# Windowed attention with a two-layer MLP: the fourth tile of keys and queries transposed by DMA instead of on the tensor engine

## Chip, cores and metric

The kernel runs on one core of a Trainium2 chip. The metric is the time of one execution on the device in microseconds, as the median of several runs. The profile is of one such execution.

## What is computed

Attention over a band of 32 tokens to either side, for 8 sequences of 576 tokens and 8 heads of 64 values; then, on the 4608 tokens with the heads side by side, a layer of width 2048 with a quick GELU, and a layer back to 512. All inputs and the output are float32.

```python
scores = scale * np.matmul(q, k.transpose(0, 1, 3, 2))          # (8, 8, 576, 576), scale 1/8
mask = np.abs(pos[:, None] - pos[None, :]) <= 32
scores = np.where(mask, scores, -1000000000.0)
attn = softmax(scores)
x = np.matmul(attn, v)                                          # then to (4608, 512)
h = x @ w_in
out = (h * (1.0 / (1.0 + np.exp(-1.702 * h)))) @ w_out
```

## The kernel before

The tokens of all sequences are one row of 4608. Keys and queries are handled in tiles of 512 tokens (the first 576 tokens are the two pieces "A" and "B", then come tiles 1, 2, 3 and so on). Attention is done in units of 128 query tokens, 36 of them, each shifted by 32 tokens, so that unit u takes queries 128u+32 to 128u+159 and keys 128u to 128u+191. The MLP takes pairs of units, 256 tokens, called t. The instructions of every engine stand in the order in which the code writes them; nothing reorders them afterwards. Each engine works through its own list and waits on semaphores.

`head()` is the opening: loads, and the attention and MLP of the first units. From `window(4)` on one window does one pair: window w computes the attention of units 2w and 2w+1, the first MLP layer of pair w-1 (`layer1(w - 1, d)`, eight pieces), and the second layer of pair w-2. Window 4 is written out by hand, since there the opening meets the steady state: it does units 7, 8 and 9, the rest of the second layer of units 4 and 5, and the first layer of pair 3.

Scores need keys and queries with the 64 values of a head on the partitions. They are held in rings: `kT`, 1536 tokens and 64 more, and `qT`, 384 columns for each of four token phases and 16 more. Tile 3 starts again at the front of the ring (token 1536 is place 0). A unit that reads over the ring's end finds the first tokens repeated behind it; these are copied there by VectorE, for queries in `queries_wrap` (L226), for keys as the tile is put in place (in `keys_T`, or by the copy at L741). Unit 11 is the first that reads tile 3, in its second block, through these repeated places.

Two ways lead into the rings:

- By TensorE (`keys_T`, `queries_T`): the tile is loaded by `load_heads`, four consecutive tokens of a head on one partition; `pair_heads` copies two heads side by side into `kc` or `qc`; `heads_T` transposes in four groups of four into one PSUM bank, and a copy (L106) puts it into the ring. Tiles A, B, 1, 2 and 3 go so.
- By DMA (`keys_X`, `queries_X`): keys are loaded by `load_keys`, a token on a partition, 128 tokens at a time, and each 128 tokens are one transposing transfer (`dma_start_transpose`) from the sync engine's queue. Queries are loaded by `load_heads`, copied by `pair_heads`, and then moved by one transposing transfer for the tile. Tiles 4 to 8 go so, issued in `feed`: in an even window the first two key transfers of a tile, in the odd window after it the query transfer and the two other key transfers.

All loads from memory go out on the queue of GpSimd, which casts to bf16. The sync engine's queue carries the stores of the output, the transposing transfers of `kT` and `qT`, and those of x (`x_T` without a bank, L315). Both queues keep their order of issue, and a transfer waits for the eighth transfer before it on its side. Staging buffers `ks` and `qs` are three deep. PSUM banks come in four kinds: two "h", one "o", four "a", one "t".

Other names used later: `odd_v(m)` copies the values of unit m shifted by half a unit, from `ve` to `vo` (two copies); `x_T(7, "t", nc.scalar)` transposes x of unit 7 on TensorE and copies it on ScalarE, and the first layer of pair 3 starts when this copy is done; `g_sums`, `product`, `keep`, `result` are the second layer of later pairs, with seven products in place of eight.

Of the kernel before, what the change touches and what calls it, by code (L numbers as in the profile page):

```python
# [22 lines left out]
JT = 4  # L23
NV = 8
RING = 1536
# [3 lines left out]
class _Kernel:  # L29
# [410 lines left out]
    def head(self):  # L440

        nc, dve, act, pool = self.nc, self.nc.vector, self.nc.scalar, self.nc.gpsimd
# [125 lines left out]
        self.load_v(8)  # L568
        self.load_v(9)
        self.load_v(10)  # L570
        for c in "kq":
            self.load_heads(3, c)
        self.layer1(2, 0)
        self.values(6)
        self.norm(6)
# [15 lines left out]
            self.load_v(m)  # L591
        self.load_keys(4)
        self.load_heads(4, "q")

    def window(self, w):
        nc, dve, sp = self.nc, self.nc.vector, self.nc.sync
        a, b = 2 * w, 2 * w + 1
        att = w < self.NW
        t, act = w - 2, nc.scalar
        l1 = [(lambda d=d: self.layer1(w - 1, d)) for d in range(8)] if w <= self.NW else []  # L600

        def run(lst, n=1):
            for _ in range(min(n, len(lst))):
                lst.pop(0)()

        def loads():
            for m in (2 * w + 6, 2 * w + 7):
                if m < self.NU:
                    self.load_v(m)
            if w % 2 == 0 and 512 * (w // 2 + 3) < self.N:  # L610
                self.load_keys(w // 2 + 3)
                self.load_heads(w // 2 + 3, "q")

        if w == 4:
            l2 = [(lambda u=u, i=i: self.layer2(u, i, "oh"[u % 2], (dve, act)[u % 2])) for u in (4, 5) for i in range(4)]
            self.scores(7)
            self.scores(a)
            run(l2, 3)
            self.band(7)
            self.scores(b)  # L620
            run(l2)
            self.band(a)
            self.values(7, "th")
            self.gelu_table()
            for m in (10, 11):
                self.odd_v(m, act)
            self.band(b)
            self.norm(7)
            run(l2, 2)
            self.values(a)  # L630
            self.values(b)
            run(l2)
            self.x_T(7, "t", nc.scalar)
            self.norm(a)
            self.x_T(a)
            self.norm(b)
            self.x_T(b)
            run(l2)
            loads()
            run(l1, 2)  # L640
            for c in "qk":
                for hp in range(4):
                    self.pair_heads(c, 3, hp, dve)
            run(l1, 2)
            for hp in range(4):
                self.keys_T(3, hp)
                self.queries_T(3, hp, "a", nc.scalar)
                run(l1)
            self.g_sums(w - 1, 0)
            self.feed(w)  # L650
            return
        loads()
        if not att:
            self.close(w, l1)
            return
        self.scores(a)
        if w > 5:
            self.scores(b)
        self.g_sums(t, 1, (0, 1))
        self.product(t, 1, "o")  # L660
        self.keep(t, 1, dve)
        self.product(t, 2, "h")
        if w == 5:
            self.scores(b)
        self.g_sums(t, 1, (2, 3))
        self.result(t, 11)
        self.gelu_table()
        self.product(t, 5, "t")
        self.band(a)
        self.product(t, 6)  # L670
        self.band(b, 0)
        self.keep(t, 6, dve)
        self.band(b, 1)
        run(l1)
        self.values(a)
        self.values(b)
        self.norm(a)
        self.x_T(a)
        self.product(t, 7)
        self.keep(t, 7, dve)  # L680
        self.result(t, 22)
        run(l1, 1)
        self.product(t, 4)
        self.result(t, 21, act)
        self.norm(b)
        self.x_T(b)
        self.product(t, 3)
        self.result(t, 12)
        run(l1, len(l1) - 4)
        self.g_sums(w - 1, 0)  # L690
        self.feed(w)
        run(l1, 4)
# [109 lines left out]
```

## Time and profile before

| | |
|---|---|
| median of 3 runs | 296.21 us (295.53 to 297.52) |
| the profiled execution | 295.53 us, of which the span from first to last instruction is 293.6 us |
| mean granted clock of TensorE | 1.000 |
| transposes in the chain, `tp L176` | 2% of the span |
| window 4, tile 3's transposes | 74.97 to 80.25 us |
| window 5, first scores | 80.25 us |

"Busy" is the time in which an engine has an instruction in work. The chain of work that ended last is followed back from the last instruction to what released each step. In lists of instructions or pieces the first number is the start and the second the duration, in us from the start of the span. SPq is the queue of the sync engine, whose entries are the issues of transfers: their duration is the issue and not the transfer; the landing time counts from the issue's start to the transfer's semaphore.

### The profile page before, as it was taken

The page shows a single profiled execution, that of the slowest core. Times are in us where ns is not written, and L with a number is a line of the kernel's source. Part 1 is how long each engine was busy: PE and PEld are TensorE (multiplying, and loading weights), DVE is VectorE, ACT ScalarE, POOL GpSimd, SP SyncE. Part 2 cuts the span into 40 slices and gives each one's busy share as a digit, 9 for nine tenths or more (in the row PEclk, how much of TensorE's full clock was granted, in tenths as well). Part 3 has the DMA queues.
Part 4 walks back from the last instruction along what each step waited for, and adds up shares of the span by engine and source line. Part 5 has one row for each costly group of instructions (what it writes and reads, how often), then busy time and mean ns, then how long its engine had stood idle before and what let it go on. Part 6 is the DMA issues. An engine that isn't in the chain of part 4 may idle for free.

```text
span 293.6 us, 9587 instructions
## 1 busy us (share of the span) xinstructions
PE 287.0 (98%) x4050; PEld 236.8 (81%) x4052; DVE 194.1 (66%) x584; ACT 189.6 (65%) x314; POOL 87.1 (30%) x127
## 2 busy tenths in 40 slices
PE   8899999999999999999999999999999999999994
PEld 3568765866888888888888888888888888888884
DVE  3662377679696858685868586858685858583352
ACT  4677457688775757575757575757575757675330
POOL 8875434977546202720252030202000000000000
PEclk9999999999999999999999999999999999999999
DMA  9999999999999993999299938791863030303012
GB/s 147 144 206 207 199 184 169 165 168 186 165 160 155 162 215 80 144 188 212 33 164 191 200 29 136 115 177 11 136 120 97 14 98 18 95 15 94 2 71 74
DMA packets 118650, 37.78 MB, mean 129 GB/s; under 512 B 96080, under 2 KB 114256, under 8 KB 118608
## 3 DMA queue, kind: packets, MB, share of 16 engines
q0 software_dynamic: 75888, 18.16, 71.9%
q1 hardware_dynamic: 42272, 18.62, 31.4%
q8 instruction: 32, 0.52, 0.7%
q10 hardware_dynamic: 448, 0.39, 0.5%
q14 instruction: 10, 0.08, 0.1%
HBM read 36.96 MB, written 9.44 MB: 158 GB/s over the span
## 4 chain that ended last, share of the span: by engine, by line
PE 93%; DVE 2%; DMA 1%; POOL 1%; issue 1%; ACT 0%; POOLq 0%; DVEq 0%
PE h_ps L332 43%; PE o_ps L394 32%; PE o_ps L344 7%; PE pv L292 4%; PE sc L263 4%; PE tp L176 2%; DMA ve<-in_v_dram 1%; PE tp L319 1%; DVE x L304 1%; POOL neg L237 0%; PE sc L245 0%; DVE o_sb L412 0%; POOL ve L157 0%; DVE kT L106 0%; ACT qT L106 0%
## 5 line engine op out<-in xcount | busy, mean ns | idle before, releaser
L332 PE MATMUL h_ps<-xT,w_in_sb 128*128 128x256 bf16 x1152 | 135.7, 273 | 0.0
L334 ACT ACTIVATE g<-h_ps 128x512 f16<-128x512 f32 x144 | 85.5, 595 | 73.3 <-PE h_ps L332 72.0
L332 PEld LDWEIGHTS <-w_in_sb 128*128 128x128 bf16 x1152 | 112.0, 98 | 13.4 <-issue 0.3
L157 POOL DMA_DIRECT2D ve<-in_v_dram x40 | 33.8, 855 | 99.8 <-PE pv L292 79.0
L394 PEld LDWEIGHTS <-gs 128*128 128x128 f16 x480 | 45.8, 98 | 5.8
L394 PE MATMUL o_ps<-w_sum,gs 128*128 128x256 f16 x360 | 44.3, 273 | 0.0
L269 ACT ACTIVATE p<-sc 128x512 bf16<-128x512 f32 x72 | 37.2, 603 | 2.7 <-PE sc L263 2.5
L394 PEld LDWEIGHTS <-g 128*128 128x128 f16 x360 | 34.2, 98 | 4.5 <-ACT g L334 0.2
L371 DVE TENSOR_TENSOR gs<-g 128x512 f16<-128x512 f16 x30 | 12.7, 422 | 31.6 <-ACT g L334 31.6
L304 DVE TENSOR_TENSOR x<-pv,rec 128x256 bf16<-128x256 f32 x72 | 30.6, 425 | 2.7 <-DVE rec L303 0.2
L394 PE MATMUL o_ps<-w_out_sb,g 128*128 128x256 f16 x240 | 29.0, 273 | 0.0
L412 DVE TENSOR_TENSOR o_sb<-o_ps,part 128x256 f32<-128x256 f32 x45 | 19.0, 423 | 12.0 <-PE o_ps L394 11.4
L106 DVE COPY part<-o_ps 128x256 f32<-128x256 f32 x45 | 19.1, 424 | 11.6 <-PE o_ps L394 10.3
L281 DVE TENSOR_TENSOR p<-p,mask 128x512 bf16<-128x512 bf16 x64 | 24.4, 424 | 0.6 <-ACT p L269 0.5
L344 PE MATMUL o_ps<-w_out_sb,g 128*128 128x512 f16 x96 | 23.2, 380 | 0.0
L106 DVE COPY vo<-ve 64x528 bf16<-64x528 bf16 x61 | 18.6, 305 | 3.5 <-DMA ve<-in_v_dram 2.1
L146 POOL DMA_DIRECT2D ks<-in_k_dram x22 | 18.8, 873 | 2.1 <-DMA qs<-in_q_dram 1.3
L269 ACT ACT_TABLE_LOAD x15 | 19.2, 1283 | 0.3
L431 ACT ACT_TABLE_LOAD x15 | 19.2, 1283 | 0.3
L303 DVE RECIPROCAL rec<-pv 128x4 f32<-128x4 f32 x72 | 12.6, 175 | 9.9 <-PE pv L292 9.9
L106 DVE COPY kT<-tp 128x512 bf16<-128x512 bf16 (+3 forms) x24 | 12.3, 531 | 7.3 <-PE tp L176 6.8
L292 PEld LDWEIGHTS <-p 128*64 128x64 bf16 x576 | 11.1, 110 | 6.3 <-DVE p L281 3.6
(69 smaller groups left out, 263.5 us busy)
## 6 DMA issues: line engine op xcount, KB each, us to landing
out_dram<-o_sb SPq DMA_DIRECT2D x34, 256.0 KB, 2.9
ve<-in_v_dram POOLq DMA_DIRECT2D x32, 128.0 KB, 5.9
ks<-in_k_dram POOLq DMA_DIRECT2D x19, 128.0 KB, 7.7
w_in_sb<-in_moe_w_in_dram POOLq DMA_DIRECT2D x4, 512.0 KB, 10.8
w_out_sb<-in_moe_w_out_dram POOLq DMA_DIRECT2D x4, 512.0 KB, 12.3
qs<-in_q_dram POOLq DMA_DIRECT2D x2, 448.0 KB, 11.5
qs<-in_q_dram POOLq DMA_DIRECT2D x3, 256.0 KB, 6.9
qs<-in_q_dram POOLq DMA_DIRECT2D x2, 384.0 KB, 10.8
```

The costliest lines, as they stand in the source:

```text
L106: (eng.copy if eng is self.nc.scalar else eng.tensor_copy)(out, in_)
L157: self.nc.gpsimd.dma_start(self.ve[m % NV][off:off + n, :, :self.D], self.v[b, :, s:s + n, :].rearrange("h s d -> s h d"))
L269: nc.scalar.activation(p[:, eo].rearrange("k h (s j) -> k h s j", j=JT), sc[eo].rearrange("k h (j s) -> k h s j", j=JT), AF.Exp, scale=sel ...
L281: self.nc.vector.tensor_mul(pv, pv, msk.to_broadcast([128, 4, 2, SQ]))
L292: nc.tensor.matmul(acc[half][blk * 64:blk * 64 + 64, hh, :], p[:, h % 2, h // 2 * 2 + blk, :], vt[:, h, :D + 1], start=(hh == 0), stop=(hh ...
L304: nc.vector.tensor_mul(x[:, hs, :], acc[half][:, :, :D], rec[:, hs, :].to_broadcast([128, 4, D]))
L332: nc.tensor.matmul(hps[:, i, :], self.w_in_sb[:, kr, ff * 128:(ff + 1) * 128], self.xT[t][:, kr, :], start=(i == 0 and kr == 0), stop=(i = ...
L334: nc.scalar.activation(self.g[t][:, ffs[0]:ffs[1] + 1:ffs[1] - ffs[0], :], hps, AF.Gelu_apprx_sigmoid)
L344: nc.tensor.matmul(o_ps, self.g[t][:, ff, s * 128:(s + 1) * 128], self.w_out_sb[:, ff, :], start=(ff == 0), stop=(ff == self.NFF - 1))
L394: nc.tensor.matmul(self.part[t, key], x, y, start=(first and k == 0), stop=(k == 7), skip_group_check=True)
L412: self.nc.vector.tensor_add(dst, self.part[t, src], self.part[t, other])
L431: self.nc.scalar.activation(self.spark, self.spark, AF.Gelu_apprx_sigmoid)
```

## The change

Tile 3 takes the way by DMA. Its keys are loaded by `load_keys` (five transfers on GpSimd's queue instead of two), and four transposing transfers on the sync queue, issued at the end of `head()`, put them into `kT`. Its queries are still loaded by `load_heads`; ScalarE copies them in window 4, where it had copied the values of units 10 and 11, and one transposing transfer, issued after the loads of window 4, puts them into `qT`. VectorE copies the first 64 keys behind the ring's end and then the values of units 10 and 11. TensorE's 32 transposes, the eight copies before them and the twelve after them are gone, and the eight pieces of the first layer follow one another.

```diff
@@ head()
         self.load_v(8)
         self.load_v(9)
         self.load_v(10)
-        for c in "kq":
-            self.load_heads(3, c)
+        self.load_keys(3)
+        self.load_heads(3, "q")
         self.layer1(2, 0)
...
         self.load_keys(4)
         self.load_heads(4, "q")
+        for c in range(JT):
+            self.keys_X(3, c)
@@ window(), w == 4
             self.gelu_table()
-            for m in (10, 11):
-                self.odd_v(m, act)
+            for hp in range(4):
+                self.pair_heads("q", 3, hp, act)
             self.band(b)
...
             run(l2)
             loads()
-            run(l1, 2)
-            for c in "qk":
-                for hp in range(4):
-                    self.pair_heads(c, 3, hp, dve)
-            run(l1, 2)
-            for hp in range(4):
-                self.keys_T(3, hp)
-                self.queries_T(3, hp, "a", nc.scalar)
-                run(l1)
+            self.queries_X(3)
+            dve.tensor_copy(self.kT[:, :, RING:], self.kT[:, :, 0:64])
+            for m in (10, 11):
+                self.odd_v(m, dve)
+            run(l1, 8)
             self.g_sums(w - 1, 0)
             self.feed(w)
             return
```

## The prediction

> **What bounds the kernel now.** I read the busy times and the chain of the page first, then the chain and timeline from 50 to 92 us, where the change lies, then the sync engine's queue and the landing times there.
>
> ```profile
> PE 287.0 (98%) x4050; PEld 236.8 (81%) x4052; DVE 194.1 (66%) x584; ACT 189.6 (65%) x314; POOL 87.1 (30%) x127
> DMA  9999999999999993999299938791863030303012
> PE 93%; DVE 2%; DMA 1%; POOL 1%; issue 1%; ACT 0%; POOLq 0%; DVEq 0%
> ```
>
> TensorE is busy for 98% of the span and carries 93% of the chain that ended last. It has next to no idle time to lose, so only work taken off it, or a stall put into it, moves the end. The DMA row says that the 16 engines are near full in the first 15 slices, 110 us: a transfer added there is not free.
>
> The chain over the end of window 4 and the start of window 5 (start, us, what):
>
> ```profile
> 71.32 3.65 PE h_ps L332 x32
> 74.97 0.45 PE tp L176 x8
> 75.42 0.87 PE h_ps L332 x8
> 76.29 0.45 PE tp L176 x8
> ...
> 79.38 0.87 PE h_ps L332 x8
> 80.25 0.37 PE sc L263 x32
> 80.63 1.85 PE o_ps L394 x16
> 82.48 0.38 PE sc L263 x32
> ```
>
> The pieces touch. Four pieces "tp L176" are the transposes of tile 3. At 80.25 the scores of unit 10 start, at 82.48 those of unit 11, and these are the first to read tile 3: unit 11 is tokens 1408 to 1535, its second block's queries run to token 1567, and tile 3 begins at 1536. They read it through the wrap copy of the query ring on VectorE:
>
> ```profile
> 81.39 0.19 DVE L226 COPY qT<-qT 128x128 bf16<-128x128 bf16 x1
> ```
>
> The sync queue in the same time, and then the first transfer of the kind that the change adds:
>
> ```profile
> 70.70 2.70 SPq L315 DMA_TRANSPOSE xT<-x  x2
> 73.49 0.55 SPq L349 DMA_DIRECT2D out_dram<-o_sb  x1
> 74.14 4.71 SPq L151 DMA_TRANSPOSE kT<-ks  x2
> ...
> 95.95 6.24 SPq L221 DMA_TRANSPOSE qT<-qc  x1
> ```
>
> Landing times from the issue's start, each from the DMA answer of a short window: the first xT at 70.70, the two kT from 74.14 on, the qT at 95.95:
>
> ```profile
> xT<-x SPq DMA_TRANSPOSE x1, 8.0
> ...
> kT<-ks SPq DMA_TRANSPOSE x1, 8.8
> ...
> kT<-ks SPq DMA_TRANSPOSE x1, 9.8
> ...
> qT<-qc SPq DMA_TRANSPOSE x1, 10.8
> ```
>
> And over all five qT transfers:
>
> ```profile
> DMA to landing us min/median/max: 4.4/8.3/10.8
> ```
>
> What to see: a transposing transfer issued near 74 us needs 8 to 10 us, though the fastest of its kind needs 2.4.
>
> [...] on the chain eight pipelined transposes take 0.45 us, and a transfer of four such tiles lands after 2.4 to 9.8 us. [...] the qT at 95.95 landed after 10.8 us, one at 212.8, with the loads nearly over, after 4.4. [...] the granted clock is 1.000 throughout[...].
>
> **The change part by part.**
>
> *Off TensorE.* 32 transposes in four groups of 0.45 us: 1.8 us less. The eight products of layer 1 between them keep their 0.87 us each; ScalarE then gives one 0.60 us activation per product and keeps up. The scores of unit 10 move from 80.25 to 78.45, those of unit 11 from 82.48 to 80.7. This is all that the change can win (the 0.3 us wait before 71.32 aside).
>
> *Off VectorE and ScalarE.* VectorE loses eight copies of 0.31 us and four pairs of 0.82 us (5.8 us), and gets four vo copies of 0.305 us and a ring copy of 0.21 us. ScalarE loses four qT copies of 0.58 us and four vo copies of 0.65 us, and gets four qc copies. A ScalarE copy of this size from SBUF is not shown; the nearest rows are vo (0.63 us) and the casts from q_raw (0.62 us), so 4 x 0.62 = 2.5 us in place of 2.6 us. Both engines have room, so I count nothing.
>
> *ScalarE's new wait.* The qc copies stand at 68.2 us and wait for the queries of tile 3. In before these were issued up to 57.75 and landed after 9.2 us, at 66.95. Now five key loads of 0.87 us stand ahead in place of two of 0.69 us, so they are issued about 3 us later (59 to 61.5); but they queue in the DMA engines anyway, and there the key tile is 4096 runs of one token and head in place of 1024 runs of four tokens. The trace's packets give about 1150 short ones or 375 long ones per us: 3.6 us in place of 2.7. Landing is then about 68[...]. Behind the qc copies on ScalarE is the xT copy for which layer 1 at 71.32 waits; it would be up to 2.3 us late. I take 0, since the wait below contains it.
>
> *Keys.* Four kT transfers, issued as the pieces land, about 62 to 67. The ring copy on VectorE at 72 waits for the first. They are hidden, but they load the sync ring ahead of the store and the two xT. The xT are wanted only at 82.9 (84.71 less 1.8) and landed near 80: cover of about 3 us. Later GpSimd loads shift by 1 to 5 us; v11 and v12, wanted at 72 by the vo copies, landed at 67.8 and 68.7, which is thin but enough.
>
> *Queries, the step that decides.* The qT transfer stands behind the two xT and the store, so it is issued at about 74.1, where kT was. The kT issued there, with a quarter of its packets (512 against 2048), landed 8.8 us later, at 83.0; the second, another 512 behind it, at about 85.2. The other 1536 packets take 1.8 us at the rate of the undisturbed transfer at 212.8 (about 850 per us), or 6.6 us at the 2.2 us per 512 seen between the two kT. So qT lands between 84.8 and 89.6; I take the middle, 87.2. The wrap copy waits for it on VectorE, and behind that the sums and copies of window 5. Add 0.2 us for the copy and 0.2 for the two hand-overs: unit 11's scores go on at 87.6 in place of 82.48, 5.1 us late, after TensorE has been idle from 80.7. Nothing makes this up, as later windows are full.
>
> *Clock after the stall.* [...] bounds 0 and 3.4. I take 1.7. The knock-on of VectorE's delayed work falls in this slow stretch, so I add nothing.
>
> Sum: 5.1 + 1.7 = 6.8 us (the 1.8 us gained are already in the 80.7). On the profiled execution's 295.53 us (span 293.6 and 1.9 around it) that is 302.3; the median of the runs shown is 0.7 above, so 303.0.
>
> **The rivals.**
>
> *Transfer in time, no stall.* If qT lands by 80.3, 6.2 us after issue, the scores of unit 11 never wait and the change gains 1.8 us: 294.4. For it: two of five qT landed after 4.4 and 4.8 us, and the code keeps the qT far ahead in all later windows. Against it: those two ran when the loads were nearly over, and in this very place a transfer of a quarter of its size took 8.8. It decides the sign at a landing of about 82.1, the point where the stall eats the 1.8 us.
>
> *Short stall.* A landing at the median of 8.3 us, 82.4, lets the scores go on at 82.8: 0.3 us late[...], 296.5. For it: the GpSimd queue may hold less at 75 us than before, as its issues are paced by landings. Against it: the kT landings again, and three transfers in the ring ahead.
>
> *Backlog.* The four kT fill the sync ring[...], so the store and both xT land late, and qT at 92: 9.9 us and 1.7 for the clock, 307.8. For it: two kT in a row took 4.71 us to issue, so the ring does fill. Against it: it has 6 us to drain before 74.
>
> *ScalarE decides.* If qs lands at 70.5 and qT is in time, layer 1 starts 2.3 us late and the gain is gone: 296.7. It only counts beside the first rival.
>
> **How the numbers follow.** The forecast has 0.62, with its own range from 298.9 (landing 84.8, no clock loss) to 307.1 (89.6 and 3.4 us). Backlog 0.10, short stall and ScalarE together 0.20, no stall 0.08. The range 295.5 to 307.5 leaves out the no-stall case and the far end of the backlog. One per cent, 3 us, is about what a measurement can tell. Faster by that needs more than the 1.8 us that TensorE gives up, so 0.04 for something unseen; within 1%: no stall and the short ones, 0.25; slower: 0.71.
>
> **What would show it.** In the profile after: no tp pieces after 74 us in the chain; scores of unit 10 near 78.5; a wait of TensorE near 81 to 87 on VectorE's wrap copy (L226's line), which itself waits on the qT transfer; landing of that transfer over 10 us; a granted clock below 1 just after. I am wrong if the qT transfer lands within 8 us of its issue, or if TensorE stalls before layer 1 of tile 3 by more than at unit 11.

## The result, and the profile after

The changed kernel takes 307.03 us, the median of 4 runs (306.87 to 309.45), beside 296.06 us of the kernel before in the same session: a ratio of 1.0381, with a 95% interval of 1.0318 to 1.0445. Some executions of every kernel here run slower as a whole; the medians are of all executions, the ratios of the others alone, so that a ratio can differ from that of two medians. The profiled execution took 307.04 us, with a span of 305.3 us and a mean granted clock of 0.978.

The lines of the page that answer to those shown of before: busy time by engine, the granted clock and the DMA engines' share in 40 slices (of 7.63 us here), and the shares of the chain that ended last:

```profile
PE 289.1 (95%) x4018; PEld 236.8 (78%) x4020; DVE 190.6 (62%) x573; ACT 187.6 (61%) x310; POOL 89.1 (29%) x130
...
PEclk9979999999966999999999999999999999999999
DMA  9999996999999999499969977792944030303012
...
PE 88%; DMA 7%; DVE 2%; ACT 1%; issue 1%; POOL 0%; SPq 0%; POOLq 0%; DVEq 0%
```

TensorE has 32 instructions fewer but is busy 2 us longer, since the clock falls in the 12th and 13th slice (and once early, in the third). The chain has now 7% of DMA, where it had 1%: 5% are a query transfer, 2% a load in the opening. The chain of waits from 73 to 102 us (start, us, what) shows the query transfer:

```profile
73.16 1.76 PE h_ps L332 x16
74.92 0.02 issue
74.94 0.61 ACT g L334
75.55 0.23 SPq L349
75.78 0.05 issue
75.83 15.36 DMA qT<-qc
91.19 0.02 issue
91.22 0.21 DVE qT L226
91.42 0.04 issue
91.46 0.59 PE sc L263 x19
92.06 3.53 PE o_ps L394 x16
95.58 1.65 PE h_ps L332 x8
97.23 0.63 PE pv L292 x32
97.86 0.98 PE o_ps L394 x8
98.84 0.87 PE h_ps L332 x8
99.72 1.75 PE o_ps L394 x16
101.46 5.24 PE h_ps L332 x48
```

The query transfer is issued at 75.83 and lands 15.4 us later. VectorE's wrap copy (L226) goes on at 91.22, TensorE's scores of unit 11 at 91.46. The waits between 60 and 110 us (us in total, times, longest) name the same pair:

```profile
DVE qT L226 <- DMA qT<-qc: 12.3, 1, 12.3
...
PE sc L263 <- DVE qT L226: 8.9, 1, 8.9
```

After it the same 16 products that take 1.85 us in the kernel before take 3.53 us, and eight products of layer 1 take 1.65 us instead of 0.87: half clock, a granted clock of 0.50 from 86.8 to 97.0 us. From 98.84 on all pieces have their old lengths, and no wait of TensorE on a transfer comes after this one.

In the kernel before the scores of unit 10 start at 80.25 and those of unit 11 at 82.48; after them its chain goes on so:

```profile
82.86 1.85 PE o_ps L394 x16
84.71 0.87 PE h_ps L332 x8
85.58 0.63 PE pv L292 x32
86.22 0.98 PE o_ps L394 x8
87.20 0.87 PE h_ps L332 x8
88.07 1.75 PE o_ps L394 x16
89.82 5.24 PE h_ps L332 x48
```

Set side by side by where a piece starts, the difference of the two spans is complete:

| piece | before | after | later by | added since the row above |
|---|---|---|---|---|
| first transposes of x of unit 4 | 50.01 | 51.90 | 1.9 | 1.9: in the opening, whose code is the same up to here |
| scores of unit 10 | 80.25 | 80.08 | -0.2 | -2.1: the transposes gone from TensorE, and some 0.2 us of waits among the products |
| scores of unit 11 (after: all but the first four products) | 82.48 | 91.46 | 9.0 | 9.2: the wait for the query transfer |
| 48 products of layer 1 | 89.82 | 101.46 | 11.6 | 2.6: half clock after the wait |
| end of the span | 293.6 | 305.3 | 11.7 | nothing |

Of the 1.9 us of the opening, 0.4 come from a late copy on VectorE (0.58 us in place of 0.19, at 16.4 us) and 1.5 from 3.4 us at half clock from 18.5 to 21.9. No instruction of the change has run by then, and executions of the kernel before fall into two groups too, most of them near 296 us with a mean clock of 1.00 or near 297.5 us with 0.994, which is what one such stretch of 3.4 us gives. So the change itself costs about 9.7 us in this profile. All four executions of the changed kernel have a mean clock of 0.977 or 0.978, as much half clock as the profiled one; whether the early stretch is among them in all four isn't known, and if it is, up to 0.6% of the ratio is not shown to be the change's.

### The profile page after: what moved, and what is told of

Its sections match the earlier page's. It is cut to its first block, busy times and chain, and to the rows that moved or that the text cites. A ratio compares the mean times of both kernels' runs of the same rounds, so it can differ in the third digit from the quotient of the medians.

```text
span 305.3 us, 9518 instructions
## 1 busy us (share of the span) xinstructions
PE 289.1 (95%) x4018; PEld 236.8 (78%) x4020; DVE 190.6 (62%) x573; ACT 187.6 (61%) x310; POOL 89.1 (29%) x130
## 4 chain that ended last, share of the span: by engine, by line
PE 88%; DMA 7%; DVE 2%; ACT 1%; issue 1%; POOL 0%; SPq 0%; POOLq 0%; DVEq 0%
PE h_ps L332 40%; PE o_ps L394 30%; PE o_ps L344 7%; DMA qT<-qc 5%; PE pv L292 4%; PE sc L263 4%; DMA qs<-in_q_dram 2%; PE tp L176 1%; PE tp L319 1%; DVE x L304 1%; ACT qT L106 0%; PE sc L245 0%; PE junk L437 0%; DVE o_sb L412 0%; DVE kT L106 0%
## 5 line engine op out<-in xcount | busy, mean ns | idle before, releaser
L332 PEld LDWEIGHTS <-w_in_sb 128*128 128x128 bf16 x1152 | 113.0, 99 | 14.2
L394 PEld LDWEIGHTS <-gs 128*128 128x128 f16 x480 | 46.5, 99 | 6.6
L394 PE MATMUL o_ps<-w_sum,gs 128*128 128x256 f16 x360 | 46.0, 279 | 0.0
L269 ACT ACTIVATE p<-sc 128x512 bf16<-128x512 f32 x72 | 37.3, 603 | 11.6 <-PE sc L263 11.5
L106 DVE COPY part<-o_ps 128x256 f32<-128x256 f32 x45 | 19.1, 424 | 12.9 <-PE o_ps L394 11.7
L146 POOL DMA_DIRECT2D ks<-in_k_dram x27 | 22.7, 868 | 7.5 <-DMA ks<-in_k_dram 5.5
L263 PE MATMUL sc<-qT,kT 64*64 64x64 bf16 x1152 | 14.8, 197 | 9.1 <-DVE qT L226 8.9
L263 PEld LDWEIGHTS <-kT 64*64 64x64 bf16 x1152 | 12.2, 109 | 13.6 <-issue 13.3
L106 DVE COPY vo<-ve 64x528 bf16<-64x528 bf16 x65 | 19.3, 297 | 2.3 <-DMA ve<-in_v_dram 0.8
```

What stands on the lines that cost most here:

```text
L106: (eng.copy if eng is self.nc.scalar else eng.tensor_copy)(out, in_)
L146: self.nc.gpsimd.dma_start(kn[off:off + n, c], self.k[b, :, s:s + n, :].rearrange("h s d -> s h d"))
L263: nc.tensor.matmul(sc[eo][lo:lo + 64, 2 * hp + blk, :], self.kT[r, hp, at:at + 64], self.qT[r, JT * hp:JT * hp + JT, q0:q0 + 16], start=(s ...
L269: nc.scalar.activation(p[:, eo].rearrange("k h (s j) -> k h s j", j=JT), sc[eo].rearrange("k h (j s) -> k h s j", j=JT), AF.Exp, scale=sel ...
L332: nc.tensor.matmul(hps[:, i, :], self.w_in_sb[:, kr, ff * 128:(ff + 1) * 128], self.xT[t][:, kr, :], start=(i == 0 and kr == 0), stop=(i = ...
L394: nc.tensor.matmul(self.part[t, key], x, y, start=(first and k == 0), stop=(k == 7), skip_group_check=True)
```

## The experiments

Two theories. **Theory A**: only the query transfer at unit 11 is late, and a kernel in which that one wait is gone is as fast as before or faster. **Theory B** (theory D in the later expectations, where the room in the engines is named as what counts): the DMA engines have no room in the first 100 us, so the transfers that the change adds come out as a late transfer somewhere, whichever it is. Theory C of the first expectation gives the opening's 1.9 us to the change. The line numbers of all kernels lie within a few of those of the changed one.

### Keys alone by DMA

Against the changed kernel, the queries go back to TensorE, and ScalarE again copies the values of units 10 and 11:

```diff
-            for hp in range(4):
-                self.pair_heads("q", 3, hp, act)
+            for m in (10, 11):
+                self.odd_v(m, act)
...
-            self.queries_X(3)
             dve.tensor_copy(self.kT[:, :, RING:], self.kT[:, :, 0:64])
-            for m in (10, 11):
-                self.odd_v(m, dve)
-            run(l1, 8)
+            run(l1, 2)
+            for hp in range(4):
+                self.pair_heads("q", 3, hp, dve)
+            run(l1, 2)
+            for hp in range(4):
+                self.queries_T(3, hp, "a", nc.scalar)
+                run(l1)
```

> Tile 3's keys by DMA as in the changed kernel, its queries by TensorE as before. Theory A (the late qT transfer alone makes the loss): no wait of TensorE at unit 11, no half-clock stretch near 90 us, and 16 transposes less, so 295 us, 1 us below before. Theory B (the added key runs and kT transfers crowd the DMA engines and make other data late): still several us slower than before, 299 or more. Theory C (the 1.9 us that the changed kernel had already lost by 50 us in its profile belongs to the change): 297, with that loss seen before 50 us again.

306.07 us (302.22 to 308.46), ratio 1.0205 (1.0125 to 1.0285). In the profile the wait at unit 11 is gone and another has come. Waits of the stretch:

```profile
PE h_ps L332 <- ACT xT L106: 4.8, 1, 4.8
ACT vo L106 <- DMA ve<-in_v_dram: 4.8, 1, 4.8
```

and in its chain

```profile
62.02 11.96 DMA ve<-in_v_dram
```

The load of values issued at 62.02 lands 12 us later; ScalarE's copy of them stands ahead of the copy of x, and layer 1 starts late, after which the clock is 0.53 between 75 and 82 us; a second wait, of 3.6 us, follows for the x issued at 116 us. This profile is of the execution that took 308.46 us. The ratio rests on those of 302.22 and 304.31 us, whose mean clocks of 0.994 and 0.993 stand for some 3.6 and 4.2 us at half clock, where the 0.983 of the profile stands for 10.4; that they waited at the same places is not shown. But they too are slower than before, and no query transfer is concerned: theory A alone doesn't hold. Nor does theory C: in this profile and in the next there is no half clock near 20 us (1.00 from 18 to 24 us), and both kernels are slower all the same.

### Queries alone by DMA

Against the changed kernel, the keys are loaded by `load_heads` and transposed on TensorE between the products of layer 1:

```diff
-        self.load_keys(3)
-        self.load_heads(3, "q")
+        for c in "kq":
+            self.load_heads(3, c)
...
-        for c in range(JT):
-            self.keys_X(3, c)
...
-            dve.tensor_copy(self.kT[:, :, RING:], self.kT[:, :, 0:64])
             for m in (10, 11):
                 self.odd_v(m, dve)
-            run(l1, 8)
+            run(l1, 2)
+            for hp in range(4):
+                self.pair_heads("k", 3, hp, dve)
+            run(l1, 2)
+            for hp in range(4):
+                self.keys_T(3, hp)
+                run(l1)
```

> Tile 3's queries by DMA as in the changed kernel, its keys by TensorE and in two loads as before. Theory A: the qT transfer is issued at about 74 us again and lands after 11 to 15 us, unit 11 stalls 5 to 9 us, and the clock falls to half after it: 302 to 307 us. Theory B: with the four kT transfers and the short key runs gone the qT lands as those of later windows do, after some 8 us, and the loss is under 2 us: 296 to 298.

304.7 us (303.43 to 305.26), ratio 1.0247 (1.0196 to 1.0298).

The chain, then the waits:

```profile
74.75 14.54 DMA qT<-qc
```

```profile
PE sc L263 <- DVE qT L226: 6.8, 1, 6.8
```

With none of the four key transfers and with the shorter key loads, the query transfer still takes 14.5 us. The two halves cost about 2% each, and together 3.8%; but in the profiles, where the changed kernel lost 1.9 us in the opening and this one did not, the queries alone cost as much as both (304.96 us beside 307.04 less 1.9).

### TensorE kept busy through the wait

Against the changed kernel, 38 products that nobody reads before the scores of unit 11:

```diff
         if w == 5:
+            self.keep_busy(38, "t")
             self.scores(b)
```

> The changed kernel with 38 idle products of 0.216 us (8.2 us) put on TensorE just before the scores of unit 11, in the time in which it stood still. If the half clock after the stall costs 2 to 3 us by itself, this removes it: 304 to 305 us, with the granted clock at 1.0 after 91 us. If the slow stretch after the stall is not the clock's but comes of waits on VectorE and ScalarE, the time stays at 307. If the idle products themselves reach past the landing, 308.

310.18 us (307.0 to 312.77), ratio 1.0402 (1.0323 to 1.0481): nothing gained. The profiled execution is the longest of the four. The table of stretches (length; busy us of TensorE, its weight loads, VectorE, ScalarE, GpSimd; clock; DMA share and GB/s):

```profile
82.00:92.00 10.00, 8.63 (x45) 3.86 (x43) 0.23 (x2) 1.08 (x2) 2.31 (x4) 1.00 1.49 154
92.00:100.00 8.00, 7.73 (x119) 6.68 (x119) 6.77 (x22) 4.14 (x7) 4.62 (x7) 1.00 2.57 137
```

The clock stayed at 1.00, but then VectorE set the pace: the chain runs from its wrap copy through what was queued behind it, sums and copies, to

```profile
94.10 1.00 DVE p L281 x3
...
95.82 0.41 PE pv L292 x14
96.23 0.98 PE o_ps L394 x8
```

The last of these starts at 97.86 in the changed kernel, so 1.6 of the 2.6 us are won here. This execution then waits 4.7 us for the x issued at 118 us. The execution of 307.0 us had a mean clock of 1.000, so no half clock anywhere, and took as long as the changed kernel, which has 13.7 us of it. Where that time went instead is left open, as it was not profiled; the profile shows that the half clock and VectorE's backlog lie side by side.

### The changed kernel without the loads of tile 5

In window 4 the loads of tile 5's keys and queries are left out; later reads use tile 4's buffers, so the output lacks tile 5.

```diff
             if w % 2 == 0 and 512 * (w // 2 + 3) < self.N:
+                if w == 4:
+                    for c in "kq":
+                        self.stage[c, 5] = self.stage[c, 4]
+                    return
                 self.load_keys(w // 2 + 3)
```

> The changed kernel without the loads of tile 5's keys and queries in window 4 (tile 4's are used in their place, so the output of those units is another): 4096 short and 1024 long runs less on the DMA engines while the qT transfer is in flight. If the turns of these loads are what holds the qT transfer up, it lands after 8 to 10 us in place of 15.4, unit 11 waits 2 to 4 us in place of 9, and the time is 299 to 302 us. If the transfer is slow by itself or by what stands ahead of it in the sync queue, it still takes over 13 us and the time stays near 306.

304.35 us (302.99 to 305.27), ratio 1.0256 (1.0205 to 1.0306).

```profile
74.27 14.16 DMA qT<-qc
```

With those loads gone the transfer still takes 14.2 us, and TensorE still waits 7.8 us. So it is not these loads that hold it. Two x and a store are still issued ahead of it on its queue, at 70.90 and 73.65, and the page's DMA row (slices of 7.53 us) still has a 9 in both slices from 75.3 to 90.4 us, the 11th and the 12th:

```profile
DMA  9999998998997999699999969691954030303012
```

The edit took loads away, but it did not empty the engines in that stretch. How much of the 14.2 us is due to what was issued before it is not shown.

### Queries first

Against the changed kernel, tile 3's queries are loaded before its keys, copied by VectorE at the end of the opening and transposed there, ahead of the keys; ScalarE copies the values as before.

```diff
-        self.load_keys(3)
         self.load_heads(3, "q")
+        self.load_keys(3)
...
+        for hp in range(4):
+            self.pair_heads("q", 3, hp, dve)
+        self.queries_X(3)
         for c in range(JT):
             self.keys_X(3, c)
```

> The changed kernel with the loads of tile 3's queries ahead of its keys, the copies into qc on VectorE at the end of the opening, and the qT transfer issued there, ahead of the four kT, so about 10 us sooner; ScalarE keeps the values of units 10 and 11. Theory A: qT lands by about 78 us, before unit 11 asks for it, no stall, and the 1.8 us of transposes are won: 294 to 295 us. Theory B: ten transfers of the tile in the crowded stretch delay the x transfers or the values, and it stays at 298 or more.

303.32 us (301.54 to 305.13), ratio 1.0227 (1.0165 to 1.0289). Unit 11 no longer waits. The sync queue (start, us, line, what, number):

```profile
64.71 4.40 SPq L221 DMA_TRANSPOSE qT<-qc  x1
69.21 5.75 SPq L151 DMA_TRANSPOSE kT<-ks  x4
75.05 0.53 SPq L349 DMA_DIRECT2D out_dram<-o_sb  x1
75.69 4.73 SPq L315 DMA_TRANSPOSE xT<-x  x2
```

and the wait that came of it

```profile
PE h_ps L332 <- DMA xT<-x: 5.4, 1, 5.4
```

Taking the query transfer ahead moves the two transfers of x from 70.70 (before) to 75.69; the second of them lands 9.4 us after 78.71, and TensorE waits 5.4 us for it. Theory A's remedy for its wait moves the wait to the next user of the queue.

### The kernel before, with its keys loaded in short runs

One token and head per run instead of four tokens, 4096 runs instead of 1024, and nothing else:

```diff
-        for c in "kq":
-            self.load_heads(3, c)
+        kn = self.stage["k", 3] = self.work.tile([128, self.H, JT * self.D], BF16, name="ks", tag="ks", bufs=3)
+        for j in range(JT):
+            for off, b, s, m in self.pieces(*self.tokens(3)):
+                self.nc.gpsimd.dma_start(kn[off // JT:(off + m) // JT, :, j * self.D:(j + 1) * self.D],
+                                         self.k[b, :, s + j:s + m:JT, :].rearrange("h p d -> p h d"))
+        self.load_heads(3, "q")
```

> The kernel before, with tile 3's keys loaded into the same places by eight transfers of one-token runs (4096 runs) in place of two of four-token runs (1024). Nothing else differs. Theory D (the DMA engines are full until about 95 us, and whatever is added makes some later transfer late): the loads behind it land 1 to 4 us later, the vo copies of units 10 and 11 on ScalarE or the copies of tile 3 wait for them, 297 to 300 us. Theory A (only the position of the qT transfer costs): 296 us.

303.44 us (299.31 to 303.79), ratio 1.0197 (1.0114 to 1.028). The loads alone cost about what the keys' half of the change costs. In the profile TensorE waits 2.5 us for an x issued at 112.16 and 1.6 us for a query transfer; some 2 us are again lost in the opening, where the page's clock row has a 7 in the third slice, from 15.1 to 22.7 us. The execution of 299.31 us had a mean clock of 1.000; it is only some 3 us above the kernel before, so part of this 2% is half clock.

### The kernel before, with four spare key transposes

Four transfers at the end of the opening into a buffer that nobody reads:

```diff
+        self.spare = self.work.tile([128, 4, 4, 128], BF16, name="kc", tag="kc")
+        for c in range(4):
+            self.nc.sync.dma_start_transpose(self.spare[:, c],
+                                             self.stage["k", 3][:, 2 * c:2 * c + 2].rearrange("p h d -> p (h d)"))
```

> The kernel before, with four spare transposing transfers of the size of the kT ones, from tile 3's keys into a buffer that nobody reads, at the end of the opening. No instruction waits for their data. Theory D: they [...]stand ahead of the store and the two x transfers in the sync queue, so values of units 11 and 12 or x of units 8 and 9 come late: 298 to 302 us, with a wait of TensorE behind a vo copy near 71 us or behind an x transfer near 85. Theory A: 296 us.

303.41 us (301.57 to 306.93), ratio 1.0207 (1.0133 to 1.0281). The expectation was wrong on one point, that no instruction waits for them: the buffer came from the place of `kc`, and VectorE's next copy into that place had to wait for the transfer:

```profile
DVE kc L106 <- DMA kc<-ks: 5.9, 1, 5.9
...
PE tp L176 <- DVE kc L106: 4.3, 1, 4.3
```

So this run mixes a wait that the edit made itself with the load on the engines, and decides nothing between the theories.

### The kernel before, with one spare query transpose

One transfer of the size of the query transfer, where the change has it, into a free buffer; the kernel before does all else:

```diff
             loads()
+            spare = self.work.tile([128, 16, 128], BF16, name="qc", tag="qc")
+            sp.dma_start_transpose(spare, self.stage["q", 3].rearrange("p h d -> p (h d)"))
             run(l1, 2)
```

> The kernel before, with one spare transposing transfer of the size of the qT one, into a buffer that nobody reads, in the place where the changed kernel issues its qT. It lands late as there (over 12 us), but nobody waits for it. Theory A: with the wait gone no cost, 296 us, so the loss of the changed kernel's query part is wholly the wait. Theory D: the loads of tile 5 and of values land later and a later window waits: 298 us or more.

301.85 us (301.27 to 305.35), ratio 1.0207 (1.0118 to 1.0295). No instruction waits for this transfer. The only new wait, 4.6 us, lies some 40 us later, in the chain and the waits:

```profile
107.81 10.75 DMA xT<-x
```

```profile
PE h_ps L332 <- DMA xT<-x: 4.6, 1, 4.6
```

In the kernel before that x is issued at about the same time, 107.51, and lands after 4.3 us instead of 10.8. What lies between shows in the loads issued from 74 to 112 us (what, number, KB each, median us to landing), first before, then with the spare transfer:

```profile
qs<-in_q_dram POOLq DMA_DIRECT2D x1, 320.0 KB, 11.9
```

```profile
qs<-in_q_dram POOLq DMA_DIRECT2D x1, 320.0 KB, 16.3
```

Each load lands later, and each issue on GpSimd's queue waits for the eighth load before it: in the trace of the kernel before none comes sooner than 0.28 us after that load's landing. The two query loads of tile 6 are issued from 99.90 on instead of 91.69, and the x of window 6 meets them. In the DMA row the slice from about 110 us on (the 16th), the first with room, has a 3 before and a 9 here:

```profile
DMA  9999999999999999999699979592953030303012
```

One transfer that is not used costs a wait of 4.6 us at a place 40 us away. The span is 6.3 us longer than before; the other 1.7 us match what 3.4 us at half clock, from 119.3 on, cost. This is theory B without anything of the change's own waits.

### The keys' transfers split

Against the kernel with queries first, only the first key transfer, which the repeated places need, stays at the end of the opening; the other three go behind the transfers of x. VectorE copies the values of units 10 and 11, as in the changed kernel.

```diff
         self.queries_X(3)
-        for c in range(JT):
-            self.keys_X(3, c)
+        self.keys_X(3, 0)
...
-            for m in (10, 11):
-                self.odd_v(m, act)
...
             loads()
+            for m in (10, 11):
+                self.odd_v(m, dve)
             dve.tensor_copy(self.kT[:, :, RING:], self.kT[:, :, 0:64])
+            for c in range(1, JT):
+                self.keys_X(3, c)
```

> Tile 3 by DMA, put in the best order I can find: its queries loaded first, copied on VectorE and sent with the first key piece at the end of the opening; only these are wanted by unit 11. The three other key pieces follow after the x transfers of units 8 and 9, and the values of units 10 and 11 are copied on VectorE. Theory D (what is added to the full DMA engines comes out as some late transfer): x of units 8 and 9 or unit 11's queries still late, 298 to 302 us. Theory A' (only the order on the sync queue costs): no wait, 294 to 295 us.

301.73 us (301.11 to 303.12), ratio 1.016 (1.012 to 1.0199). The x of units 8 and 9 is in time now, and two later ones are late, the second of window 5 and the second of window 6:

```profile
89.44 10.82 DMA xT<-x
108.92 10.10 DMA xT<-x
```

TensorE waits 1.4 and 4.0 us for them. In this kernel too the order on the sync queue decided who is late, not whether someone is.

### The same, with later loads

Against the last kernel, the loads of tiles 5 to 8 come two windows later:

```diff
-            if w % 2 == 0 and 512 * (w // 2 + 3) < self.N:
-                self.load_keys(w // 2 + 3)
-                self.load_heads(w // 2 + 3, "q")
+            if w % 2 == 0 and w > 4 and 512 * (w // 2 + 2) < self.N:
+                self.load_keys(w // 2 + 2)
+                self.load_heads(w // 2 + 2, "q")
```

> The kernel of e12 with the loads of tiles 5 to 8 issued two windows later each, so that 4096 short and 1024 long runs leave the stretch from 75 to 95 us. Theory D: with this room x of units 8 and 9 lands in time and the 1.8 us of transposes are won, 294 to 296 us. If it stays above 298, room alone is not what is missing, and the transposing transfers are slow among the remaining loads too.

297.31 us (20 runs, 295.49 to 301.67) beside 297.33 us of the kernel before: ratio 1.0006 (0.9984 to 1.0027). The x at 89 us lands after 7.4 us instead of 10.8, and nothing waits for it. What is left:

```profile
108.93 6.37 DMA xT<-x
```

```profile
PE h_ps L332 <- DMA xT<-x: 1.7, 1, 1.7
```

The first line is of the chain, the second of the waits: window 6 now holds the postponed loads, and TensorE waits 1.7 us there, where it waited 4.0. That is as much as TensorE saved.

### The kernel before with the later loads alone

The edit of the last kernel, made to the kernel before.

> The control for e13: the kernel before with only the loads of tiles 5 to 8 two windows later. Nothing waits for them in before, so 296 us, with shorter landing times of the x transfers of units 8 and 9 (about 5 us in place of 8). If the later loads collide with windows 6 to 10, 298 or more.

296.16 us (12 runs, 295.53 to 299.18), ratio 0.9999 (0.9968 to 1.003). In the kernel before the later loads win nothing. So in the kernel above they gave the 1.6% back together with the new transfers, and not by something of their own. One point of the expectation failed: the x of units 8 and 9 landed after 8.8 and 9.0 us, not after 5 (before: 8.0 and 8.2). The room shows in later transfers: the x of window 6 issued at 106.86 lands after 2.6 us, where before it took 4.3.

### The later loads spread over two windows

Against the kernel with split keys and later loads:

```diff
-            if w % 2 == 0 and w > 4 and 512 * (w // 2 + 2) < self.N:
-                self.load_keys(w // 2 + 2)
-                self.load_heads(w // 2 + 2, "q")
+            i = (w + 4) // 2
+            if w > 5 and 512 * i < self.N:
+                self.load_keys(i, (2, 3) if w % 2 else (0, 1))
+                if w % 2:
+                    self.load_heads(i, "q")
```

> The kernel with the split key transposes and later loads, its loads of tiles 5 to 8 spread over two windows: half of the keys in an even window, the other half and the queries in the odd one after it, so that at most half a tile of loads stands beside the transfers of x in a window. Nothing is left out of the computation. Theory D (the engines' room is what counts): the transfers of x for units 12 and 13 are in time, the wait at the sixth window's x goes, and what the products no longer spend on the fourth tile's transposes shows in the total: 1 to 2 us below the kernel before, about 295. Rival: spreading only moves the crowd, an x is late again in one of the windows, or the opening itself still holds the 1.8 us: equal to before within 0.3 per cent, or slower by 1 us.

296.78 us (22 runs, 294.42 to 300.38) beside 297.23 us: ratio 0.9991 (0.9964 to 1.0018). The rival has it: equal to before. Its profiled execution took 300.38 us, far above the median, so only the place of its wait is read: it is again the x of window 6,

```profile
106.29 9.82 DMA xT<-x
```

for which TensorE waits 2.8 us. In this execution half a tile of loads beside the query and key transfers of tile 4 still went with a late x; that the others waited there too is not shown. No version that was run beats the kernel before.

## Why the prediction was right

**The deciding step held.** Slower, by a wait of VectorE's wrap copy for the query transfer and of TensorE behind it, then a lower clock: that is what the profile shows, at the place named. The query transfer was issued at 75.83, 73.9 without the opening's 1.9 us (predicted 74.1). It landed at 91.2, 89.3 on the same footing: inside the 84.8 to 89.6 of the forecast, at its far end and not in its middle, 87.2. The total came out near the end of the stated range as well, and the opening's 1.9 us, which the forecast knew nothing of, are part of that.

**The sizes, term by term.** The sum was 302.3 us for the profiled execution; it took 307.0, 4.7 more. Three terms make this up, to within 0.2 us:

- The landing, 2.1 us, of which 2.0 reach the scores. The rate was well taken: the trace's packet records have nearly all of the transfer's 2048 packets between 83.7 and 89.5, 350 per us, so 1536 of them in 4.4 us, where the estimate was 4.2, the middle of 1.8 and 6.6. What was too early is the start. The estimate let the first 512 packets land with the kT of the kernel before, 8.8 us after issue; that one's packets began 5.8 us after its issue, those of the query transfer 7.9, behind the two transfers of x and the store.
- The clock, 0.9 us: 2.6 instead of 1.7, inside its bounds of 0 and 3.4. The 1.7 and the bounds were the author's estimate; the profile of the kernel before, with a clock of 1.000 throughout, does not show them. In the changed kernel TensorE is idle from 82.5 us to the restart at 91.46; the granted clock is 1.00 up to 86.8 and 0.50 from there to 97.0, 10.2 us, and 1.00 again after it. So half clock lasted 5.6 us beyond the restart, in which TensorE was busy throughout. Half of 5.6 is 2.8 us, near the 2.6 that the pieces show.
- The opening, 1.9 us: not foreseen, and over before any instruction of the change.

**What was costed at nothing.** The gain of 1.8 us on TensorE came, 2.1 with the short waits among the products. ScalarE's copies of the queries did not wait: 0.54 us each from 69.96 on, without idle time before them; the delay of up to 2.3 us that was named for them, the author's estimate, did not come. The kT transfers were hidden: VectorE's ring copy stood at 73.53 without a wait. The cover of the values of units 10 and 11, called thin, held in the changed kernel, where VectorE copies them at 73.78. The run with keys alone has ScalarE read them earlier, and in its profile it did not hold.

**The rivals.** A transfer in time and a short stall fell with the landing of 15.4 us. The backlog rival had a landing near 92 by a late store and late transfers of x. Part of it is there: the last packet of the four kT moved at 74.9 (73.0 without the opening), and the two x landed 9.6 us after issue where they had taken 8.0 and 8.2. But they were in time, and with no kT at all (queries alone) the query transfer still took 14.5 us. The size of the total came out close to its 307.8, but by the three terms above.

**What the prediction did not see.** It treated the loss as one late transfer. The experiments show the wait at unit 11 to be the form that the loss takes in this order of issues: with that wait taken away in three ways (keys alone, queries first, split keys) the kernel still lost 1.6 to 2.3%, in the profiles each time at another transfer, and one spare transfer in the kernel before lost 2.1%. The sentence "a transfer added there is not free" in its first part was the wider truth, and it was not carried through into a price. It takes both, order and room: order alone (split keys) left 1.6%; fewer loads in the changed kernel's own order left 2.6%; split keys with later loads left nothing to within 0.3%. The 1.8 us of TensorE are not won either.

What stays open: why the kernel with TensorE kept busy had no lower total, and how much of each 2% is the half clock that follows a wait. One profile divides it, that of the spare query transfer, with 4.6 us of wait and 1.7 of half clock; for the other kernels no run separates the two.

## What to carry to other kernels

Where the DMA row is full, moving work from the bounding engine to a transfer trades 1.8 us of sure work for a place in a queue, and the price appears at whichever transfer has the least cover, perhaps 40 us later. Before such a move, price it by adding the transfer alone, unread, to the old kernel, into a buffer that nothing else waits for; one run shows the cost without the change. Reordering the queue here only chose the victim, and fewer loads alone left the victim waiting; what helped was both, and the loads moved elsewhere have to be worth more than what they in turn make late.

## What the runs showed of the hardware

- Loads and transposing transfers moved side by side in near equal numbers of packets: in the changed kernel the records have 368 short load packets (128 bytes) and 392 transposing ones from 84 to 85 us, 385 and 405 in the next us, 377 and 403 in the third. With loads alone 1138 such packets moved from 60 to 61 us. So in these three us, beside the query transfer of 2048 packets, the short loads went at a third of that rate, a price that the prediction lacked.
- A query transfer issued behind others on its queue, into full engines, moved its first packets late: 4.5 us after issue for the one at 95.95 in the kernel before, about 8 us for the one at 75.83 after, against 1.2 us for the one at 212.8 in the kernel before, when the loads were nearly over.
- The clock fell to half for 3.4 us in the opening in some executions of the same code: in the changed kernel from 18.5 to 21.9 us, and with TensorE kept busy to a mean of 0.72 from 18 to 24 us, where keys alone, queries alone and queries first have 1.00. In the changed kernel TensorE was busy for 69% of the 3.4 us ahead of it (2.33 of 3.40 us from 15.1 us on), in the kernel before for 81% of the same 3.4 us (2.77), and there the clock stayed at 1.00. What makes it fall is not shown. With the late copy it cost 1.9 us here, as much as this change could win.
